# A gated spectral filter beside a two-layer network on one core: new tile blocks, smaller second-layer pieces and a new order of work

## The chip, the cores and the metric

The kernel runs on one core of one Trainium2 chip. The metric is device time in microseconds (us) of one execution; a lower number is better. The kernel before took 148.89 us as the median of 3 runs (148.78, 148.89 and 149.5). Engines are called PE (TensorE, matrix products), DVE (VectorE), ACT (ScalarE), POOL (GpSimd) and SP (SyncE, which here only issues DMAs).

## The reference

The input x has 2048 rows of 640 numbers. Each row is normalized; the normalized matrix goes through a filter in the frequency domain and through a two-layer network, and both results are added to x.

```
def _A_ref(x, w_r, w_i):
    B, S, D = x.shape                                   # 1, 2048, 640
    X = rfft2(x.astype(float32), axes=(-2, -1))
    X = X * (w_r + 1j * w_i)                            # 2048 x 321 weights
    return irfft2(X, s=(S, D), axes=(-2, -1)).astype(bfloat16)

def _B_ref(x, w1, b1, w2, b2):
    h = gelu(einsum("bsd,df->bsf", x, w1) + b1)         # 640 -> 1536
    return einsum("bsf,fd->bsd", h, w2) + b2            # 1536 -> 640

xn = _layernorm(x)
return x + _A_ref(xn, A_w_r, A_w_i) + _B_ref(xn, B_w1, B_b1, B_w2, B_b2)
```

## The kernel before

The 2048 rows are 16 tiles of 128 rows; tile c holds the rows 16p + c of partition p. Everything lies in SBUF at fixed places, PSUM is 8 banks of 512 fp32 columns.

A small planner records every operation with what it reads and writes (`Plan.op`), and two hand-kept tables then fix everything: `ORDER` lists all operations as engine:name, which is the order of each engine's instructions, and `SLOTS` says which of a pool's buffers or PSUM banks each name uses. `Plan.sync` puts in the semaphore waits that these need. An operation waits before its first instruction for all earlier users of its buffers. Nothing is reordered on the chip: an operation that waits holds up all that stands behind it on its engine.

The names in the table, in the order of the data:

- `x`, `w1_hj` (W1 in ten pieces: half h of its 1536 columns, 128-row piece j), `w2_h`, `W..` (the filter), `e`, `m`, `n`, `i`, `g`, `h` (constant tables): loads, all issued by SP one behind the other.
- `st`, `ag`, `ve`, `sq`, `rs`, `nm`: statistics, reciprocal root and normalization of a tile (DVE, the roots on ACT for tiles 0 and 1, on POOL later). `tp`/`tc`: transposition of a normalized tile on PE and its copy to `xnT` (tiles 0 to 5); `td`: the same by a DMA transpose (tiles 6 to 15).
- `h<block>.<fc>.<j>`: first layer, W1 as the stationary operand, a block of tiles from `BLOCKS` as the moving one; `ge`: the gelu on ACT, from PSUM to `gT`. In blocks 0 and 1 (one tile each) a group `h<block>.<q>.<j>` is three 128-column matmuls and needs only piece j of W1.
- `f1`, `f2` (DVE) and `G` (PE), `gx`: folding of a tile and the first step of the transform over rows, copied to `XV`.
- `b` (PE, six groups of 2 or 3 from `GROUPS`), `xb`: transform over columns; its four PSUM banks are emptied by two copies `xb.0` and `xb.1`. `c`, `y`: second step over rows, copied to `Y`. `m`, `z`: products with the filter (into `T`) and their sums (into `Z`), on DVE. `d`, `u`: the first step back, copied to `U`; `vt`: 16 DMA transposes issued by SP, from `U` back to `XV`.
- `e`, `yo`, `y2`, `yf`: transform back over columns (PE), copy and unfolding (DVE). Each `e` needs all 16 `vt`.
- `l`: second layer of a tile into PSUM, `fin`: the last step back over rows added onto it, `os`: plus x and the bias (DVE), `out`: store. For the tiles in `KEEP` the second layer is done early (`k`), added to x (`kk`) and held, and `fin` comes later on its own.
- `xs`: x plus the second bias, `idle0`, `idle1`: matmuls on zeros ahead of the first work.

So the transform is one long chain over PE, ACT, DVE and the DMA transposes, while `h`, `k` and `l` are work of PE that the table places in the chain's waits.

A second-layer sum of 640 columns is written as 512 and 128 columns in two banks (`halves`), evicted by one instruction of 640:

```
def halves(o0, w):
    return [(o0, 512 - o0), (512, o0 + w - 512)] if o0 < 512 < o0 + w else [(o0, w)]
```

All matmuls but the transposes are recorded at line 403, all copies out of PSUM at 413 (ACT) and 414 (DVE), so groups are told apart by their tiles.

Of the kernel before, what the change touches and what calls it, by code (L numbers as in the profile page):

```python
# [7 lines left out]
BF = dt.bfloat16  # L8
F32 = dt.float32
# [4 lines left out]
D = 640  # L14
# [230 lines left out]
BYPE = ()  # L245
# [9 lines left out]
dve:tc1.0 pe:h0.1.2 pe:h0.0.2 act:b1cp sp:g pe:h0.1.3 dve:f10.1 pe:h1.0.0 sp:x8 pe:h0.1.4 pe:h1.0.1 dve:f20.00 pe:h1.1.0 act:ge0.3 sp:x10 pe:h1.1.1
dve:f20.01 act:ge0.4 dve:f20.10 pe:h1.1.2 pe:h1.1.3 sp:x12 pe:h1.1.4 dve:st2.0 pe:h0.0.3 sp:x14 pe:h0.0.4 act:ge1.5 dve:st2.1 pe:h1.0.2 pe:h1.0.3
act:ge0.0 sp:W00m pe:h1.0.4 act:ge0.1 dve:ag2 pe:h1.2.0 dve:st3.1 pe:h1.3.0 act:ge0.2 pe:h1.3.1 sp:W10m act:ge0.5 dve:ve2 dve:st3.0 pe:h1.3.2 pool:rs2
act:ge1.4 pe:h0.2.0 dve:f20.11 act:ge1.2 sp:W12n pe:h0.2.1 dve:ag3 pe:h0.2.2 act:ge1.3 dve:ve3 pe:h0.2.3 dve:nm2 pool:rs3 pe:h1.3.3 sp:W01n pe:h1.3.4
pe:h1.2.1 pe:h0.2.4 act:ge1.10 pool:xbpad1 pe:tp2.0 pool:xbpad0 sp:w2_0 dve:nm3 act:ge1.11 pe:h0.3.0 act:ge1.9 dve:st4.0 pe:h1.2.2 sp:bias2 act:tc2.0
pe:tp3.0 dve:f11.1 pe:h1.2.3 sp:W11n pe:h1.2.4 dve:tc3.0 act:ge1.1 pe:h0.3.1 pe:h0.3.2 act:ge1.7 pe:h0.3.3 dve:f11.0 act:ge1.0 pe:h2.0.0 act:ge0.8  # L260
dve:st6.0 pe:h2.0.3 act:ge0.6 pe:h0.3.4 dve:f21.10 act:ge1.8 pe:h2.4.0 dve:st7.1 act:ge1.6 pe:h2.1.0 sp:W00n act:ge0.7 dve:st7.0 pe:G0 act:ge0.10
pe:h2.2.0 dve:st6.1 pe:h2.1.3 dve:st4.1 pe:h2.8.0 act:ge2.0 dve:st5.0 pe:h2.8.3 pe:G1 act:ge2.1 dve:f21.11 dve:f21.00 pe:h2.9.0 act:ge0.9 dve:st11.0
pe:h2.9.3 act:ge0.11 pe:h2.4.3 act:gx0.0 dve:st5.1 pe:h2.5.0 dve:f21.01 pe:h2.2.3 dve:ag4 dve:ag5 pe:h2.3.0 dve:st8.1 pe:h2.3.3 dve:ve4 dve:ag7
pe:h2.5.3 dve:ag6 pool:rs4 dve:st10.0 pe:h2.6.0 act:ge2.4 dve:ve6 pe:h2.6.3 dve:st13.0 pool:rs6 pe:G2 act:ge2.5 dve:nm4 pe:G3 act:ge2.2 dve:nm5
pe:h2.10.0 act:ge2.3 pe:tp4.0 dve:st14.1 act:ge2.9 pe:tp5.0 dve:nm7 act:tc4.0 pe:h2.10.3 dve:st9.1 pe:h2.11.0 act:tc5.0 dve:f12.0 pe:h2.11.3 pe:h2.7.0
dve:st10.1 pe:h2.7.3 act:ge2.8 dve:nm6 pe:h3.0.0 act:ge2.6 dve:ag10 pe:h3.0.3 dve:st14.0 sp:td6 pe:h3.1.0 act:ge2.7 dve:f12.1 pe:h3.2.0 act:gx1.0
dve:st8.0 pe:h3.2.3 pe:h3.3.0 dve:f22.10 sp:td7 pe:h3.3.3 dve:st9.0 pe:h3.4.0 act:ge3.3 dve:f22.01 pe:h3.4.3 dve:ag8 pe:h3.5.0 act:ge3.2 dve:f22.00
pe:h3.1.3 dve:st13.1 act:ge2.10 pe:h3.5.3 dve:f22.11 act:ge3.1 pe:h3.6.0 dve:ag9 dve:f13.1 pe:G4 act:ge3.0 dve:ve8 pe:h3.6.3 dve:f13.0 act:ge3.4
pool:rs8 pe:h3.10.0 act:ge2.11 dve:st11.1 pe:h3.10.3 pe:G5 act:ge3.5 dve:f23.01 dve:st12.0 pe:h3.11.0 act:gx2.0 dve:nm8 pe:h3.11.3 pe:h3.8.0
dve:f23.00 sp:td8 pe:h3.8.3 dve:nm9 pe:h3.7.0 dve:f23.10 act:ge3.10 pe:h3.7.3 pe:h3.9.0 dve:ag11 dve:f23.11 act:ge3.7 dve:ve10 pe:h3.9.3 dve:f14.1  # L270
# [12 lines left out]
pe:h6.4.0 act:xb2.1 dve:m1.1 pe:h6.4.3 pe:h6.5.0 pe:h6.7.3 act:xb2.0 dve:m0.0 pe:k2.6 dve:m0.1 act:ge6.7 pe:h6.5.3 pe:c1.0 act:ge6.4 dve:z1.1 pe:k2.9
# [38 lines left out]
def bass_parallel_sum__spectral_gfnet__dense_activation_gelu__prompt_kernel(  # L322
# [21 lines left out]
    with ExitStack() as es:  # L344
# [466 lines left out]
```

## Time and profile before

| what | value |
|---|---|
| timed runs | 148.78, 148.89, 149.5 us (median 148.89) |
| the profiled execution: its time, its span | 149.7 us, 148.4 us |
| PE, DVE, ACT busy | 144.8, 110.9, 82.9 us |
| PE clock granted | 1.00 throughout |
| first matmul, last matmul (start) | 0.99 us, 146.2 us |
| first `b` group, first `e` group (PE) | 47.06 us, 105.21 us |

The span runs from the first to the last instruction of the profiled execution, and 1.3 us of that execution lie outside it. Rows of the timeline read: start, length, engine, line, operation, output<-inputs, shape, count, and in brackets the idle time ahead and what ended it. A matmul's length is about 0.2 us longer than the time after which the next one starts, since matmuls overlap: the spacing is (length of a row minus the mean length of one) divided by (count minus one).

### The profile page before, as it was taken

Reading aid. Unit: us, or ns where it says so; the run is one execution under the profiler, and the core shown is the slowest. Engines: PE = TensorE matmul, PEld = TensorE weight load, DVE = VectorE, ACT = ScalarE, POOL = GpSimd, SP = SyncE. Lnnn points to the kernel's source line nnn. Section 1 sums busy time; section 2 is a strip of 40 time slices with the busy share of each in tenths; the row PEclk is TensorE's granted clock in tenths of the full one; section 3 lists DMA queues with packets and bytes.
Section 4 is the critical chain, followed back from the end, with each engine's and each line's share of the span. In section 5 each row is a group of like instructions: output and inputs, shape, how many; then the busy total and the mean of one; then the engine's idle time right before and its main releaser. Section 6 shows DMA issues by size and latency. Waiting matters only on the chain.

```text
span 148.4 us, 4311 instructions
## 1 busy us (share of the span) xinstructions
PE 144.8 (98%) x1847; PEld 99.4 (67%) x1847; DVE 110.9 (75%) x242; ACT 82.9 (56%) x161; POOL 7.0 (5%) x18
## 2 busy tenths in 40 slices
PE   7999999999999999999999999999999999999994
PEld 7989888888868766666554534345676665655564
DVE  2888999999997799498659759700098898968743
ACT  3649889998984775994555467891624204000000
POOL 2003030222200000000000000000000000000000
DMA  4899999366997993004200460645001122101333
GB/s 133 293 326 406 306 269 178 60 93 164 299 203 128 213 210 134 4 4 88 44 4 7 88 133 4 133 92 115 19 4 44 44 88 95 44 0 49 133 111 110
DMA packets 27882, 18.07 MB, mean 122 GB/s; under 512 B 18904, under 2 KB 26584, under 8 KB 27736
## 3 DMA queue, kind: packets, MB, share of 16 engines
q1 hardware_dynamic: 27840, 17.81, 48.8%
q8 instruction: 14, 0.23, 0.6%
q14 instruction: 4, 0.03, 0.1%
q10 hardware_dynamic: 24, 0.00, 0.0%
HBM read 10.92 MB, written 2.62 MB: 91 GB/s over the span
## 4 chain that ended last, share of the span: by engine, by line
PE 70%; DVE 13%; DMA 6%; SPq 5%; issue 2%; ACT 2%; POOL 1%
PE ps L403 70%; DMA X<-in_A_x_dram 6%; SPq L398 5%; DVE stats L508 4%; DVE T L564 3%; DVE T L560 2%; ACT Xb L413 2%; DVE Z L537 1%; DVE mv L510 1%; POOL rstd L519 1%; DVE T L537 1%; DVE ve L518 0%; DVE U L537 0%; DVE W L772 0%
## 5 line engine op out<-in xcount | busy, mean ns | idle before, releaser
L403 PE MATMUL ps<-xnT,W 128*128 128x256 bf16 (+2 forms) x480 | 58.7, 274 | 0.3 <-DMA W<-in_B_w_dram 0.3
L403 PE MATMUL ps<-W,gT 128*128 128x128 bf16 (+4 forms) x408 | 57.9, 291 | 0.0
L403 PEld LDWEIGHTS ps<-xnT,W 128*128 128x128 bf16 x480 | 40.2, 98 | 12.4 <-issue 1.9
L619 ACT ACTIVATE gT<-ps,b1col 128x256 bf16<-128x256 f32 (+2 forms) x96 | 39.3, 483 | 10.8 <-PE ps L403 10.6
L403 PEld LDWEIGHTS ps<-W,gT 128*128 128x128 bf16 x408 | 30.4, 98 | 22.3 <-issue 1.7
L508 DVE BATCH_NORM_STATS2 stats<-X 128x6 f32<-128x320 bf16 x32 | 14.4, 476 | 2.6 <-DMA X<-in_A_x_dram 2.6
L733 DVE TENSOR_TENSOR Wf<-Wf 128x960 bf16<-128x960 bf16 (+1 forms) x12 | 6.8, 597 | 11.8 <-ACT Wf L413 11.7
L413 ACT ACTIVATE Wf<-ps 128x960 bf16<-128x960 f32 (+1 forms) x8 | 6.9, 902 | 12.8 <-PE ps L403 12.8
L413 ACT ACTIVATE Xb<-ps 128x960 bf16<-128x960 f32 (+1 forms) x9 | 9.8, 1138 | 7.0 <-PE ps L403 7.0
L676 DVE TENSOR_TENSOR T<-Y,Wf 128x1288 bf16<-128x1288 bf16 x16 | 12.4, 824 | 0.5 <-ACT Y L413 0.4
L413 ACT ACTIVATE Y<-ps 128x644 bf16<-128x644 f32 x12 | 8.1, 715 | 3.9 <-PE ps L403 3.9
L761 DVE TENSOR_TENSOR xnT<-ps,X 128x640 f32<-128x640 f32 x8 | 6.6, 820 | 4.7 <-PE ps L403 4.7
L772 DVE TENSOR_TENSOR W<-ps,X 128x640 bf16<-128x640 f32 (+2 forms) x10 | 6.9, 687 | 3.8 <-PE ps L403 3.8
L564 DVE TENSOR_TENSOR T<-T 128x512 bf16<-128x512 bf16 (+1 forms) x32 | 9.1, 312 | 0.2
L413 ACT ACTIVATE XV<-ps 128x1280 bf16<-128x1280 f32 x7 | 8.7, 1243 | 0.1
L772 DVE TENSOR_TENSOR W<-ps,xnT 128x640 bf16<-128x640 f32 x8 | 6.5, 820 | 1.8 <-PE ps L403 1.7
L403 PE MATMUL ps<-getab,XV 32*128 32x160 bf16 (+1 forms) x128 | 7.5, 242 | 0.0
L519 POOL TENSOR_TENSOR rstd<-ve,mhalf 128x2 f32<-128x2 f32 (+1 forms) x8 | 6.1, 763 | 31.1 <-DVE ve L518 31.1
L738 DVE TENSOR_TENSOR Wf<-Wf 128x960 bf16<-128x960 bf16 (+1 forms) x12 | 6.7, 596 | 0.8 <-PE ps L403 0.7
L403 PEld LDWEIGHTS ps<-getab,XV 32*128 32x128 bf16 (+1 forms) x128 | 6.4, 146 | 1.2
L403 PE MATMUL ps<-etab,XV 32*128 32x160 bf16 (+1 forms) x128 | 7.2, 232 | 0.0
L680 DVE TENSOR_TENSOR Z<-T 128x644 bf16<-128x644 bf16 x16 | 7.0, 488 | 0.1
(52 smaller groups left out, 111.6 us busy)
## 6 DMA issues: line engine op xcount, KB each, us to landing
out_dram<-W SPq DMA_DIRECT2D x15, 160.0 KB, 1.8
X<-in_A_x_dram SPq DMA_DIRECT2D x7, 320.0 KB, 8.2
W<-in_B_w_dram SPq DMA_DIRECT2D x10, 192.0 KB, 5.6
W<-in_B_w_dram SPq DMA_DIRECT2D x2, 960.0 KB, 8.7
Wf<-in_A_w_i_dram SPq DMA_DIRECT2D x7, 160.5 KB, 3.9
Wf<-in_A_w_r_dram SPq DMA_DIRECT2D x7, 160.5 KB, 4.5
gtab<-c_G SPq DMA_DIRECT2D x1, 512.0 KB, 7.8
htab<-c_H SPq DMA_DIRECT2D x1, 512.0 KB, 5.0
```

Of the source, the lines that this page charges most:

```text
L398: return K.op(name, q, lambda e, _: e.dma_start(dst, src), reads=reads, writes=[buf], after=after, dma=sem or name, gate=gate)
L403: ins = e.matmul(o_, lhsT=lw, rhs=rh, start=st, stop=sp_, skip_group_check=True)
L413: return e.activation(dst(), src(), ACT.Copy)
L508: K.op(f"st{c}.{h}", "dve", lambda e, _, c=c, h=h: e.bn_stats(stats[:, c, 6 * h:6 * h + 6], view(X, c * D + H2 * h, [[1, H2]])), reads=[B_ ...
L519: K.op(f"rs{c0}", "pool", lambda e, _, a=a, b=b: e.tensor_tensor(out=rstd[:, a:b], in0=ve[:, a:b], in1=mhalf[:, a:b], op=ALU.pow), reads=[ ...
L564: ring_ops.append(K.op(f"f2{pair}.{k}{i}", "dve", lambda e, _, op=op, x1v=x1v, xfv=xfv, o_=o_, o0=o0, o1=o1, w=w: e.tensor_tensor(out=xfv( ...
L619: K.op(f"ge{bi}.{fc}", "act", lambda e, _, c0=c0, nt=nt, fc=fc, f0=f0, hps=hps: e.activation(gT[:, fc, 128 * c0:128 * (c0 + nt)], psb(hps. ...
L676: filt_ops.append(K.op(f"m{pair}.{k}", "dve", lambda e, _, k=k, Y=Y, TB=TB, pair=pair: e.tensor_tensor(out=view(TT, TB.slot * 8 * KP + k * ...
L680: K.op(f"z{pair}.{r}", "dve", lambda e, _, TB=TB, Z=Z, r=r, op=op: e.tensor_tensor(out=view(Zb, Z.slot * 4 * KP + r * KP, [[2 * KP, 2], [1 ...
L733: K.op(f"y2{gi}.{k}", "dve", lambda e, _, k=k, op=op, yo=yo, y2=y2, n=n: e.tensor_tensor(out=view(Wf, Y2 + y2.slot * 3 * D + (H2 - 1) * k, ...
L738: K.op(f"yf{gi}.{k}", "dve", lambda e, _, k=k, op=op, y2=y2, yf=yf, n=n: e.tensor_tensor(out=view(Wf, YF + yf.slot * 3 * D + (D - 1) * k, ...
L772: K.op(f"os{c}.{o0}", "dve", lambda e, _, c=c, os_=os_, fps=fps, o0=o0, w=w, kept=kept, base=base, home=home if kept else None: e.tensor_t ...
```

## The change

- `BLOCKS`: tiles 8 to 15 are two blocks of four instead of two blocks of two and one of four.
- The normalization of tile 0 is two instructions, columns 384 to 639 first, and the transposes and copies of each part wait for that part alone.
- The second layer, `fin`, `kk` and `os` work in pieces of 384 and 256 columns, one bank each; tile 15 keeps pieces of 320, 160 and 160.
- The product with the real filter part is written over `Y`, and the sums `z` over that; `Z` is gone. With the memory freed there are six `Y`, four `Xb` and four `U` buffers in place of two, two and three, some of them in tables that are used up by then.
- `GROUPS` are cut elsewhere (still 3, 3, 2, 3, 3, 2 tiles in some order), `idle0` has 38 matmuls instead of 42.
- `ORDER` and `SLOTS` are new in all their lines.

```diff
-BLOCKS = [(0, 1), (1, 1), (2, 2), (4, 2), (6, 2), (8, 2), (10, 2), (12, 4)]
+BLOCKS = [(0, 1), (1, 1), (2, 2), (4, 2), (6, 2), (8, 4), (12, 4)]
-GROUPS = [(0, 2), (2, 3), (5, 3), (8, 3), (11, 3), (14, 2)]
+GROUPS = [(0, 3), (3, 3), (6, 2), (8, 3), (11, 3), (14, 2)]
+CUTS = [(0, 384), (384, 256)]
-WARM = (42, 4)
+WARM = (38, 4)
...
-pe:tp0.3 sp:w1_13 pe:idle1 dve:tc0.0 dve:nm1 sp:w1_14 pe:h0.1.0 pe:h0.1.1 act:tc0.3 dve:f10.0 sp:x4 pe:h0.0.0 pe:tp1.0 sp:x6 pe:h0.0.1 pe:b1mm
-dve:tc1.0 pe:h0.1.2 pe:h0.0.2 act:b1cp sp:g pe:h0.1.3 dve:f10.1 pe:h1.0.0 sp:x8 pe:h0.1.4 ...
+dve:f10.0 pe:h0.1.0 act:tc0.3 sp:x4 pe:h0.1.1 dve:f10.1 pe:h0.1.2 act:tc1.0 pe:h0.0.0 sp:x6 pe:h0.1.3 dve:f20.01 dve:f20.10 pe:h0.0.1 act:b1cp
+pe:h0.1.4 sp:g dve:f20.00 pe:h0.0.2 pe:h1.0.0 ...
...
-        p_xn, p_x1, p_xf, p_xb, p_y, p_t, p_z, p_u = [Pool(k, n) for k, n in (
-            ("xn", 5), ("x1", 1), ("xf", 2), ("xb", 2), ("y", 2), ("t", 2), ("z", 2), ("u", 3))]
+        p_xn, p_x1, p_xf, p_xb, p_yz, p_t, p_u = [Pool(k, n) for k, n in (
+            ("xn", 4), ("x1", 1), ("xf", 2), ("xb", 4), ("yz", 6), ("t", 2), ("u", 4))]
...
+                parts = ((0, 384), (384, D)) if c == 0 else ((0, D),)
+                for (a, b), B_part in zip(parts, B_xn):
+                    norm = K.op(f"nm{c}" if not a else f"nm{c}.3", "dve", lambda e, _, c=c, n=n, a=a, b=b, xnv=xnv: e.tensor_scalar(
+                        out=xnv(n, a, [[1, b - a]]), in0=view(X, c * D + a, [[1, b - a]]), ...
...
+            m0 = K.op(f"m{pair}.0", "dve", lambda e, _: e.tensor_tensor(out=yv(Y, False), in0=yv(Y, False), in1=wv(pair, 0), op=ALU.mult),
+                reads=[Y, B_w, B_wpad], writes=[Y], after=[m1])
+                    rows = view(TT, yz(Y) + r * KP, [[2 * KP, 2], [1, KP]])
+                    return e.tensor_tensor(out=rows, in0=rows, in1=view(TT, TB.slot * 4 * KP + r * KP, [[2 * KP, 2], [1, KP]]), op=op)
...
-                            (psb(ps_.slot, [[1, b]], a - base), gT[:, fc, 128 * c:128 * c + 128], W2[:, fc, a:a + b], fc == 0, False)
-                            for fc in range(f0, f0 + 3) for a, b in halves(o0, w)],
+                            (psb(ps_.slot, [[1, w]]), gT[:, fc, 128 * c:128 * c + 128], W2[:, fc, o0:o0 + w], fc == 0, False)
+                            for fc in range(f0, f0 + 3)],
...
+                    for o0, w in CUTS:
+                        kps = K.buf(f"kps{c}_{o0}", psum, 1, HIGH)
+                        second(f"k{c}.{o0}", c, kps, o0, w, free)
...
-                for o0, w in PIECES.get(c, [(0, D)]):
+                for o0, w in PIECES.get(c, CUTS):
```

The instructions move in many places. Three of them matter here. Line 410 after the change is line 403 before it, 420 is 413, 566 is 549 and 704 is 700.

**The start, on DVE and PE.** Before, DVE up to the normalization of tile 0:

```order
L508 BN_STATS stats<-X 128x6 x3
L510 BN_AGGR mv<-stats 128x2
L508 BN_STATS stats<-X 128x6
L514 RECIPROCAL rstd<-ve 128x1
L510 BN_AGGR mv<-stats 128x2
L537 TENSOR_SCALAR Z<-X,mv,rstd 128x640
```

After it:

```order
L520 BN_STATS U<-X 128x6 x2
L522 BN_AGGR mv<-U 128x2
L520 BN_STATS U<-X 128x6 x2
L526 RECIPROCAL rstd<-ve 128x1
L522 BN_AGGR mv<-U 128x2
L552 TENSOR_SCALAR T<-X,mv,rstd 128x256
L552 TENSOR_SCALAR T<-X,mv,rstd 128x384
```

The aggregate of tile 0 stands one statistic earlier, the reciprocal stands behind the same four statistics, and the normalization is in two. On PE in the same place, before (`EB` in the new names holds the zeros and the identity that were `warm` and `ident`):

```order
L549 MATMUL ps<-ident,Z 128x128 x5
L403 MATMUL ps<-warm 128x128 x4
L403 MATMUL ps<-xnT,W 128x128 x9
L549 MATMUL ps<-ident,Z 128x128 x5
L403 MATMUL ps<-xnT,W 128x128 x3
L403 MATMUL ps<-ident,b1t 128x12
L403 MATMUL ps<-xnT,W 128x128 x84
```

and after:

```order
L566 MATMUL ps<-EB,T 128x128 x2
L410 MATMUL ps<-EB 128x12
L566 MATMUL ps<-EB,T 128x128 x3
L410 MATMUL ps<-EB 128x128 x4
L566 MATMUL ps<-EB,T 128x128 x5
L410 MATMUL ps<-xnT,W 128x128 x96
```

The transposes of tile 1 and the small bias transpose now stand ahead of all first-layer matmuls. Among these, `h0.1.4`, the first to need the fifth piece of W1, was the ninth group of three (24 matmuls ahead of it) and is the seventh (18 ahead).

**Groups 4 and 3 of the column transform, on PE and ACT.** `etab` (after: `EB`) with 24 matmuls of 160 columns is a group of three tiles. Before, PE between groups 3 and 4:

```order
L403 MATMUL ps<-etab,XV 128x160 x24
L403 MATMUL ps<-W,gT 128x512
L403 MATMUL ps<-W,gT 128x128
```

(nine such pairs in all stand there), and after, where group 4 comes ahead of group 3:

```order
L410 MATMUL ps<-EB,XV 128x160 x24
L410 MATMUL ps<-W,gT 128x384 x6
L410 MATMUL ps<-xnT,W 128x512 x5
L410 MATMUL ps<-EB,XV 128x160 x24
```

ACT has both copies of the first of the two groups there, before and after; after:

```order
L638 ACTIVATE gT<-ps,b1col 128x512
L420 ACTIVATE Xb<-ps 128x3x2x160 x2
L638 ACTIVATE gT<-ps,b1col 128x512
L420 ACTIVATE Xb<-ps 128x3x2x160
```

What stands between the two groups on PE is shorter than before.

**The DMA transposes to `XV`, on SP.** After the change the 16 of them stand in one row behind all loads:

```order
L405 DMA htab<-c_H 128x2048
L405 DMA getab<-c_GE 128x800
L704 DMA_TRANSPOSE XV<-gtab 128x5x128
L704 DMA_TRANSPOSE XV<-T 128x5x128 x2
L704 DMA_TRANSPOSE XV<-gtab 128x5x128
L704 DMA_TRANSPOSE XV<-U 128x5x128 x4
```

They stood behind the loads before as well. What differs is which instruction they wait for: the first of them needs the second copy to `U` of pair 1 (`u1.1`), and on PE all four `d` of the first four pairs now come together (`d0.0`, `d1.1`, `d0.1`, `d1.0`), behind the `c` of six pairs; before, `d0` came behind the `c` of four and `d1` some 13 us later.

More of the change, by code (lines that the diff above doesn't have):

```diff
@@ L255 @@
[L255 to L258, printed above, removed]
@@ L317 @@
[L317 to L318 removed]
+idle0:0 b1ps:0 xn0:0 x10:0 xf0:0 tps0.0:2 tps0.3:1 idle1:3 tps1.0:4 aps0:0 xn1:1 x11:0 xf1:1 tps2.0:6 tps3.0:4 aps1:0 xn2:2 x12:0 xf2:0 tps4.0:5
+tps5.0:3 aps2:0 xn3:3 x13:0 xf3:1 aps3:0 xn4:0 x14:0 xf4:0 aps4:0 xn5:1 x15:0 xf5:1 aps5:0 xn6:2 x16:0 xf6:0 aps6:0 xn7:3 x17:0 xf7:1 aps7:0 hps0_0:6
@@ L454, in first @@
             chain.append(o)
[L455 removed]
+        table.gate.append(load("bias1", "act", b1t, b1v, B_b1))
         first(load_x(0, 1))
```

359 lines of the change are left out of this document (188 added, 171 removed).

## The prediction

> **What bounds the kernel now.** I read the busy times of the engines first, then the table of waits, then PE's timeline at each place where its matmuls are not back to back.
>
> ```profile
> span 148.4 us, 4311 instructions
> PE 144.8 (98%) x1847; PEld 99.4 (67%) x1847; DVE 110.9 (75%) x242; ACT 82.9 (56%) x161; POOL 7.0 (5%) x18
> ...
> PEld ps L403 <- issue: 4.5, 19, 0.3
> ...
> PEld ps L403 <- ACT Xb L413: 1.3, 4, 0.5
> ```
>
> PE is busy for 98% of the span, and in the table of waits no other engine holds it for more than 1.3 us in all. Busy time alone proves little, since matmuls overlap, so I look at spacings:
>
> ```profile
> 28.41 1.80 PE L403 MATMUL ps<-xnT,W 128*128 128x256 bf16 x15
> 97.19 4.49 PE L403 MATMUL ps<-xnT,W 128*128 128x512 bf16 x20
> 8.97 1.24 PE L403 MATMUL ps<-xnT,W 128*128 128x128 bf16 x19 [0.27 <-DMA W<-in_B_w_dram]
> ...
> L403 PE MATMUL ps<-xnT,W 128*128 128x256 bf16 x300 | 37.0, 273 | 0.0
> L403 PE MATMUL ps<-xnT,W 128*128 128x512 bf16 x60 | 14.1, 380 | 0.0
> L403 PE MATMUL ps<-xnT,W 128*128 128x128 bf16 x120 | 8.1, 222 | 0.3 <-DMA W<-in_B_w_dram 0.3
> ```
>
> (1.80 - 0.273)/14 = 109 ns for 256 columns, (4.49 - 0.380)/19 = 216 ns for 512, (1.24 - 0.222)/18 = 56 ns for 128: PE streams columns at one rate with about 2 ns for each matmul on top. From the first transposes to the last matmul it does little else. So the change can gain only the matmuls it removes and the holes it closes, and loses every hole it opens. These are the holes that I find, beside the one in the third row above:
>
> ```profile
> 21.38 0.88 PE L549 MATMUL ps<-ident,Z 128*128 128x128 bf16 x10
> 22.10 1.15 PE L403 MATMUL ps<-xnT,W 128*128 128x256 bf16 x9
> ...
> 39.75 0.38 PE L403 MATMUL ps<-xnT,W 128*128 128x256 bf16 x2
> 40.21 0.45 PE L403 MATMUL ps<-gtab,T 128*128 128x128 bf16 x5
> ...
> 59.00 0.38 PE L403 MATMUL ps<-xnT,W 128*128 128x256 bf16 x2
> 59.64 0.50 PE L403 MATMUL ps<-Xb,mtab 32*32 32x322 bf16 x32 [0.26 <-ACT Xb L413]
> ```
>
> Ten transposes need 0.56 and took 0.72 (0.16 lost); two matmuls need 0.22 and took 0.46 (0.24 lost, at `G13`) and 0.64 (at `c1.0`: 0.42, of which some 0.1 is what any such step of 32 small matmuls costs on entry, so 0.31). Together 0.71 us, and nothing that the new order must bring back.
>
> **The change part by part.** *Matmuls.* Tiles 8 to 11 as one block: 120 matmuls of 256 columns become 60 of 512, 60 x (218 - 216) ns = 0.12 us less. Pieces of 384 and 256: the same 640 columns in two matmuls; 384 is not in the trace, between 109 and 216 ns it is half way, 163, and 163 + 109 = 272 = 216 + 56, so nothing. Tile 15's last piece:
>
> ```profile
> 144.81 0.99 PE L403 MATMUL ps<-W,gT 128*128 128x160 bf16 x12
> 145.71 0.65 PE L403 MATMUL ps<-W,gT 128*128 128x32 bf16 x12
> 146.20 0.24 PE L403 MATMUL ps<-Wf,htab 128*128 128x32 bf16 x2
> ```
>
> Six pairs of 32 and 128 columns took 0.49 us, 82 ns each; one matmul of 160 is (0.99 - 0.23)/11 = 69. Thirteen pairs save 0.17 us. The four zero matmuls less stand ahead of the first transposes, which wait for DVE: nothing. Sum: -0.29.
>
> *The start.*
>
> ```profile
> 4.27 0.19 DVE L510 BATCH_NORM_AGGREGATE mv<-stats 128x2 f32<-128x12 f32 x1
> 4.38 0.44 DVE L508 BATCH_NORM_STATS2 stats<-X 128x6 f32<-128x320 bf16 x1
> 4.82 0.16 DVE L514 RECIPROCAL rstd<-ve 128x1 f32<-128x1 f32 x1
> 5.02 0.45 DVE L537 TENSOR_SCALAR Z<-X,mv,rstd 128x640 bf16<-128x640 bf16 x1
> ```
>
> The aggregate moves ahead by one statistic, but the reciprocal still stands behind all four, so it starts at about 4.8 as before. Half of the normalization is ready some 0.2 us sooner, and tile 1's transposes fill a time in which PE had stood before. This buys nothing, since PE then waits for the fifth piece of W1, the end of the 0.27 us idle in the row at 8.97. The loads are issued in the same order, so I let it land at the same time. Then 18 first-layer matmuls are done by then and not 24; the transposes of tile 1 and the bias were done before as well. Six matmuls of 56 ns: +0.33. Bounds: 0, if the piece comes a microsecond sooner, and +0.5.
>
> *`tc3` on ACT.* The copy of tile 3 now stands on ACT behind that of tile 2, and the next 256-column matmul needs both. Before, DVE had it:
>
> ```profile
> 13.63 0.71 ACT L413 ACTIVATE xnT<-ps 128x640 bf16<-128x640 bf16 x1
> 14.13 0.48 DVE L414 COPY xnT<-ps 128x640 bf16<-128x640 bf16 x1
> ```
>
> It ends about 0.2 us after PE has run out of one-tile matmuls. +0.2 (0 to 0.4).
>
> *Evacuation in the middle.* `b` and `d` need all four low banks empty, so the two copies must fit beneath the matmuls placed between.
>
> ```profile
> 68.69 2.62 PE L403 MATMUL ps<-W,gT 128*128 128x512 bf16 x18
> 68.81 2.37 ACT L413 ACTIVATE Xb<-ps 128x960 bf16<-128x960 f32 x2 [1.87 <-PE ps L403]
> 71.23 1.12 PEld L403 LDWEIGHTS ps<-etab,XV 128*128 128x128 bf16 x24 [0.25 <-ACT Xb L413]
> ```
>
> Between groups 3 and 4, 2.55 us of matmuls just covered two copies on ACT (0.12 + 2.37 + 0.06). In the new order the cover is six matmuls of 384 and five of 512, 0.98 + 1.08 = 2.06 us, and both copies are on ACT again: a hole of 0.5 (0.1 to 0.7). By the same count ahead of `b1` (three gelus stand ahead of the second copy on ACT) about 0.25, and at `d1.1`, both copies of `d0.0` on ACT beneath twelve matmuls of 384 (1.95 us), about 0.15. Together +0.9, bounds 0.2 to 1.5. The other steps of the middle come out with 0 to 0.2 us to spare.
>
> *More evictions.* Eight `kk` and fifteen `os` become two instructions each.
>
> ```profile
> L772 DVE TENSOR_TENSOR W<-ps,X 128x640 bf16<-128x640 f32 x7 | 5.7, 819 | 1.7 <-PE ps L403 1.7
> L772 DVE TENSOR_TENSOR W<-ps,X 128x160 bf16<-128x160 f32 x2 | 0.7, 325 | 0.6 <-PE ps L403 0.6
> L772 DVE TENSOR_TENSOR W<-ps,X 128x320 bf16<-128x320 f32 x1 | 0.5, 492 | 1.4 <-PE ps L403 1.4
> ...
> 120.00:130.00 10.00, 10.00 (x99) 6.25 (x97) 8.81 (x13) 1.83 (x2) 0.00 (x0) 1.00 0.23 83
> 130.00:146.50 16.50, 16.44 (x146) 10.36 (x144) 10.72 (x18) 0.00 (x0) 0.00 (x0) 1.00 0.23 83
> ```
>
> From 160 and 320 columns: 1.04 ns a column and 158 ns fixed, of which about 80 overlap with the next one (the aggregate row above is 0.19 long and the next starts after 0.11). So a second instruction costs 0.08 to 0.16 us, 17 of them in the tail 1.4 to 2.7 us. The two rows of the tail leave DVE 1.2 + 5.8 us free. I take nothing; without that cover it is rival D. The Trainium skill (Perfetto Trace Analysis, Optimizing Scalar/DVE Operations) has a rule against this part: each VectorE instruction on PSUM carries about 125 ns, and grouping pays where the engine is saturated; by it the 17 would cost an estimated 2.1 us of DVE, inside the bounds just given.
>
> *In place.*
>
> ```profile
> L676 DVE TENSOR_TENSOR T<-Y,Wf 128x1288 bf16<-128x1288 bf16 x16 | 12.4, 824 | 0.5 <-ACT Y L413 0.4
> L680 DVE TENSOR_TENSOR Z<-T 128x644 bf16<-128x644 bf16 x16 | 7.0, 488 | 0.1
> ...
> 60.00:80.00 20.00, 20.00 (x367) 12.12 (x352) 14.29 (x24) 13.94 (x26) 0.00 (x0) 1.00 0.14 27
> 80.00:105.00 25.00, 24.99 (x355) 11.50 (x354) 13.09 (x24) 15.99 (x31) 0.00 (x0) 1.00 0.44 87
> ```
>
> `m` and `z` keep their count, shapes and types, and I take the same time for them. A slower write over an input has no row; a tenth of these 19.4 us would be 1.9 us in a middle where DVE is busy for 27.4 of 45 us.
>
> *Sum.* -0.71 - 0.29 + 0.33 + 0.2 + 0.9 = +0.4 us of span: 148.4 becomes 148.8, and the profiled time 149.7 becomes 150.1. That execution lay 0.8 above the median of its own runs, so on the median 148.9 + 0.4 = 149.3. My holes are counted where a copy just misses, and a copy that is late once leaves the next one time; I take half of the 0.4 and say **149.1**.
>
> **The rivals.** *B, the old holes go and no new ones open.* For it: the new holes are each a few tenths, less than one eviction, and the piece of W1 that I let land late may not. Against it: the table gives ACT both copies at two of the places. Then -0.71 - 0.29 = -1.0: 147.9.
>
> *C, slower: the transposes to `XV` hold up the first `e`.*
>
> ```profile
> 99.51 2.60 SPq L700 DMA_TRANSPOSE XV<-gtab  x2
> 102.15 1.28 SPq L700 DMA_TRANSPOSE XV<-U  x1
> 103.58 1.79 PE L403 MATMUL ps<-W,gT 128*128 128x512 bf16 x12
> 105.21 0.95 PE L403 MATMUL ps<-getab,XV 128*128 128x160 bf16 x12
> ...
> XV<-gtab SPq DMA_TRANSPOSE x6, 2.6
> ```
>
> Two issues take 2.64 us of SP, 1.32 each, and one lands 2.6 after its start: before, the last landed some 0.4 us ahead of the first `e`. Now all sixteen follow `u1.1` in one row: about 0.9 us from the end of `d0.1` to the end of that copy, then 15 x 1.32 + 2.6, together 23.3. Beneath it PE has, from `d0.1` to the first `e`, 60 matmuls of 512, 21 of 384, 27 of 256, a group of 0.95 and seven steps of about 0.52: 12.96 + 3.42 + 2.94 + 0.95 + 3.64 = 23.9 us. From the point where one of the copies to `U` that they wait for is over 0.6 us late, each microsecond moves the end, and nothing is left to fill it. With 1.6 us late, 149.1 + 1.0 = 150.1. Against it: DVE and ACT are busy for 13.1 and 16.0 of the 25 us there.
>
> *D, slower: DVE becomes the bound of the tail.* If the 1.4 to 2.7 us fall where `fin` waits for `yf`, half to all of the smaller figure: 149.8 to 150.5, say 150.3. Against it: the free time above.
>
> That the two-part normalization doesn't bring PE's first real work forward is my forecast already, at no cost.
>
> **How the numbers follow.** Forecast (holes close and others open, within 0.7 us of before): 0.45; B 0.25; C 0.21; D 0.09. About 0.5%, 0.74 us, is what a measurement of this kernel can tell from no change, so faster means below 148.15: B, 0.25. Within: 0.45. Slower, above 149.63: C and D, 0.30. The bounds of the unknown costs (0 to 0.5, 0 to 0.4, 0.2 to 1.5) put the forecast's own case between 148.2 and 149.9 on the median; cut where the other cases begin, its own range is 148.2 to 149.6. With B and most of C and D, cutting a tenth at either end, 147.8 to 150.4.
>
> **What would show it.** PE's first idle time in the new profile: ended by the DMA of W1, longer than 0.27 us, at 8.9. In PE's waits: `Xb` and `U` copies on ACT ahead of groups `b1` and `b3` and of `d1.1`, 0.2 to 0.5 us each. No hole at `G13`. The first `e` between 104.9 and 105.7 us with the last transpose landing just ahead of it; if it starts more than a microsecond after the last matmul ahead, C is right. In the tail PE without idle time, DVE busier by about 1.4 us. The last matmul at 146 to 147 us. The forecast is wrong if PE has over 3 us of holes in all, or under 0.7.

## The result, and the profile after

| | time, us | runs | profiled execution (span) |
|---|---|---|---|
| predicted | 149.1 (147.8 to 150.4) | | |
| kernel before | 149.0 median (148.78 to 149.5) | 6 | 149.7 (148.4) |
| changed kernel | 150.54 median (149.96 to 151.98) | 6 | 150.41 (149.1) |

The changed kernel is slower: 1.0109 of the time before, 95% interval 1.0061 to 1.0157, some 1.6 us. Every ratio here and below compares the fast runs of the two kernels alone, so it can differ a little from the quotient of two medians. The six runs of the changed kernel spread over 2.0 us and those of the kernel before over 0.7; but 11 and 21 further runs of the kernel before, beside the experiments, spread over 1.7 each (148.85 to 150.59 and 148.83 to 150.53), so the spread sets the two kernels apart no further. The first rows of the changed kernel's page:

```profile
span 149.1 us, 4174 instructions
PE 143.5 (96%) x1770; PEld 100.5 (67%) x1770; DVE 114.6 (77%) x265; ACT 79.2 (53%) x150; POOL 6.9 (5%) x24
```

PE has less to do (143.5 against 144.8) and a longer span to do it in. The table of waits names a releaser that held PE in none of the rows of before:

```profile
PEld ps L410 <- DMA XV<-U: 1.4, 1, 1.4
...
PE ps L410 <- DMA XV<-U: 1.1, 1, 1.1
...
PEld ps L410 <- DMA W<-in_B_w_dram: 0.5, 1, 0.5
...
PE ps L410 <- ACT Xb L420: 0.3, 1, 0.3
```

It is one wait, ahead of the first `e`. PE's timeline (start, duration, idle time ahead in brackets) at the places of the prediction:

```profile
6.54 1.19 PE L410 MATMUL ps<-xnT,W 128*128 128x128 bf16 x18
8.06 1.35 PE L410 MATMUL ps<-xnT,W 128*128 128x128 bf16 x21 [0.34 <-DMA W<-in_B_w_dram]
...
52.00 1.26 PE L410 MATMUL ps<-xnT,W 128*128 128x256 bf16 x10
53.24 0.93 PE L410 MATMUL ps<-EB,XV 128*128 128x160 bf16 x11
...
67.38 1.24 PE L410 MATMUL ps<-xnT,W 128*128 128x512 bf16 x5
68.94 1.25 PE L410 MATMUL ps<-EB,XV 128*128 128x160 bf16 x20 [0.32 <-ACT Xb L420]
...
76.19 1.46 PE L410 MATMUL ps<-W,gT 128*128 128x384 bf16 x8
77.58 0.51 PE L410 MATMUL ps<-T,ntab 32*32 32x320 bf16 x32
...
103.66 0.49 PE L410 MATMUL ps<-W,gT 128*128 128x256 bf16 x3
105.22 1.42 PE L410 MATMUL ps<-getab,XV 128*128 128x160 bf16 x24 [1.07 <-DMA XV<-U]
...
146.41 0.23 PE L410 MATMUL ps<-Wf,htab 128*128 128x160 bf16 x1
```

With 109 ns a matmul of 256 columns, PE was free at 103.66 + 3 x 0.109 = 103.99 and started `e0` at 105.22: **1.23 us lost**. At the other end, the last matmul starts at 146.41 and the span ends 2.7 us later; before, 148.4 - 146.20 = 2.2. The other rows are read against the prediction below.

Why the transposes are late shows in SP's timeline and in the row of landing times (for the tile `XV`) of the changed kernel:

```profile
80.69 1.25 SPq L704 DMA_TRANSPOSE XV<-gtab  x1
81.98 2.59 SPq L704 DMA_TRANSPOSE XV<-T  x2
84.61 1.28 SPq L704 DMA_TRANSPOSE XV<-gtab  x1
85.93 6.17 SPq L704 DMA_TRANSPOSE XV<-U  x4
92.15 1.61 SPq L704 DMA_TRANSPOSE XV<-T  x1
93.80 2.60 SPq L704 DMA_TRANSPOSE XV<-gtab  x2
96.44 1.28 SPq L704 DMA_TRANSPOSE XV<-T  x1
97.77 6.04 SPq L704 DMA_TRANSPOSE XV<-U  x4
```
```profile
DMA to landing us min/median/max: 2.6/2.7/4.6
```

The same row of before reads:

```profile
DMA to landing us min/median/max: 2.6/2.6/2.7
```

At 1.28 an issue and 0.03 between, four take 5.21 us; here two groups of four took 6.17 and 6.04, and a single one 1.61. That is 0.96 + 0.83 + 0.33 = 2.1 us more than sixteen undisturbed issues. The window of the DMA records from 86.0 to 90.6 us, in 40 slices of 0.115 us, shows what happens in the first of them (first row: busy tenths of the DMA engines; second: what they moved; then the queues):

```profile
DMA  9999981000399999990000000010000039999990
GB/s 218 236 220 200 198 161 29 0 0 0 76 200 209 196 203 178 60 149 0 0 0 0 0 0 0 0 9 9 9 9 9 11 62 253 285 289 292 247 237 3
...
q8 instruction: 1, 0.02, 1.3%
```

Two transposes' bursts run at about 200 GB/s. In the 18th slice, at 88.05, comes one packet of the instruction queue, 16 KB; it takes 0.96 us in its record, and for 1.6 us next to nothing is moved. The page counts 14 such packets in either kernel, one for some 126 of 1770 matmuls of the changed one, as if they carried PE's program; x2, x3 and x8 below test that. In the trace of the changed kernel they stand at 80.05, 88.05, 91.73 and 98.74 in this stretch: the first ahead of the row, three in it. In that of before they stand at 80.74, 89.55 and 97.82, each at a gap between two groups of transposes.

### The profile page after: what moved, and what is told of

Same layout as the page of the kernel before. It is cut to its first block, busy times and chain, and to the rows that moved or that the text cites. A ratio compares the mean times of both kernels' runs of the same rounds, so it can differ in the third digit from the quotient of the medians.

```text
span 149.1 us, 4174 instructions
## 1 busy us (share of the span) xinstructions
PE 143.5 (96%) x1770; PEld 100.5 (67%) x1770; DVE 114.6 (77%) x265; ACT 79.2 (53%) x150; POOL 6.9 (5%) x24
## 4 chain that ended last, share of the span: by engine, by line
PE 74%; SPq 10%; ACT 6%; DMA 5%; DVE 2%; issue 1%; DVEq 0%
PE ps L410 74%; SPq L704 8%; DMA W<-in_B_w_dram 3%; ACT gT L638 3%; DMA XV<-U 2%; SPq L405 2%; ACT Xb L420 2%; DVE W L802 2%; ACT xnT L420 1%; ACT gtab L420 0%; ACT T L420 0%; PE ps L566 0%; DVEq L224 0%
## 5 line engine op out<-in xcount | busy, mean ns | idle before, releaser
L410 PE MATMUL ps<-W,gT 128*128 128x256 bf16 (+3 forms) x396 | 59.4, 296 | 0.0
L520 DVE BATCH_NORM_STATS2 U<-X 128x6 f32<-128x320 bf16 x32 | 13.9, 474 | 2.8 <-DMA X<-in_A_x_dram 2.8
L420 ACT ACTIVATE T<-ps 128x644 bf16<-128x644 f32 (+2 forms) x17 | 9.7, 613 | 5.7 <-PE ps L410 5.7
L420 ACT ACTIVATE XV<-ps 128x1280 bf16<-128x1280 f32 (+1 forms) x8 | 9.6, 1196 | 2.8 <-PE ps L410 2.8
L802 DVE TENSOR_TENSOR W<-ps,X 128x256 bf16<-128x256 f32 (+3 forms) x17 | 7.6, 466 | 3.6 <-PE ps L410 3.4
L792 DVE TENSOR_TENSOR xnT<-ps,X 128x256 f32<-128x256 f32 (+1 forms) x16 | 7.6, 484 | 2.1 <-PE ps L410 2.1
L583 DVE TENSOR_TENSOR T<-T 128x128 bf16<-128x128 bf16 (+1 forms) x32 | 8.9, 313 | 0.1
L410 PE MATMUL ps<-Wf,htab 128*128 128x256 bf16 (+3 forms) x33 | 7.5, 295 | 0.0
L698 DVE TENSOR_TENSOR T<-T 128x644 bf16<-128x644 bf16 x16 | 7.3, 486 | 0.1
L579 DVE TENSOR_TENSOR T<-T 128x640 bf16<-128x640 bf16 x16 | 7.3, 481 | 0.1
```

What stands on the lines that cost most here:

```text
L410: ins = e.matmul(o_, lhsT=lw, rhs=rh, start=st, stop=sp_, skip_group_check=True)
L420: return e.activation(dst(), src(), ACT.Copy)
L520: K.op(f"st{c}.{h}", "dve", lambda e, _, c=c, h=h: e.bn_stats(stats[:, c, 6 * h:6 * h + 6], view(X, c * D + H2 * h, [[1, H2]])), reads=[B_ ...
L579: K.op(f"f1{pair}.{k}", "dve", lambda e, _, k=k, op=op, xnv=xnv, x1v=x1v: e.tensor_tensor(out=x1v(H2 * k, [[D, 2], [1, H2]]), in0=xnv(0, 0 ...
L583: ring_ops.append(K.op(f"f2{pair}.{k}{i}", "dve", lambda e, _, op=op, x1v=x1v, xfv=xfv, o_=o_, o0=o0, o1=o1, w=w: e.tensor_tensor(out=xfv( ...
L698: return e.tensor_tensor(out=rows, in0=rows, in1=view(TT, TB.slot * 4 * KP + r * KP, [[2 * KP, 2], [1, KP]]), op=op)
```

## The experiments

Ratios are to the kernel before, run beside each kernel; "F" is the theory of the instruction packets, "Q" that a long row backs up by itself, "U" that two of the source tensors are slow. All names stand in the order tables.

**x1_early_d0**: `d0` and its transposes ahead of `b3` and `c2`.

```
 pe:b4 ... -pe:b3 +pe:d0.0 ... +pe:d0.1 ... +pe:b3 ... pe:c2.1 ... pe:c2.0 ... -pe:d0.0 pe:d1.1 -pe:d0.1
```

> The changed kernel with d0.0 and d0.1 (and so the first four transposes to XV) ahead of b3 and c2 instead of behind them; nothing else moves on PE but the banks' users. If the unbroken row of sixteen transposes is what costs: PE's wait ahead of e0 falls from 1.1-1.2 us to under 0.5, and the time from 150.5 to 149.3-149.8 (1.002 to 1.006 of before). If the loss lies in the wait at b3, in the more numerous VectorE instructions or in the last output: e0's wait may go, but the time stays at 150.3-150.8.

151.82, 1.018 (1.0118 to 1.0242). PE did not wait for `XV` any more: six transposes were late, but the last landed at 106.81, just as PE got to `e0` (106.52 + 3 x 0.109 = 106.85). VectorE was late elsewhere: 0.46 us ahead of `d1.0` and 0.91 ahead of `b5`, both ended by copies to `U` on DVE that I had put behind its products, and 1.09 at 20 us for a normalization that the edit doesn't touch. Inconclusive: the edit made waits of its own.

**x2_phase_after**: the idle matmuls ahead of everything halved in width and doubled in number.

```
-WARM = (38, 4)        psb(b.slot, [[1, 128]]), warm, warm
+WARM = (76, 4)        psb(b.slot, [[1, 64]]), warm, warm[:, 0:64]      (idle0 alone)
```

> The changed kernel with its 38 idle matmuls of 128 columns as 76 of 64: the same PE time, 38 PE instructions more ahead of everything. Theory F (a 16 KB instruction packet of PE that meets a transpose makes it land 1.4-1.9 us late): the packets of 88.05, 91.73 and 98.74 come at about 86.3, 90.2 and 95.2, and the transposes in flight there are the late ones (those issued at about 84.6-86, 88.6-89.9 and 93.8-95), while the one issued at 97.8 lands in 2.7 us unless a packet stands there. Theory Q (a long row of transposes backs up by itself): the fifth to eighth and the thirteenth and fourteenth stay the late ones. Theory U (sources in U2 and U3): vt6, vt7, vt13 stay late. Time 149.8 to 151 under each.

151.54, 1.0154 (1.011 to 1.0198). The packets came at 86.13 and 90.19, as expected, and at 97.22, 2 us later than expected. The late transposes were the 4th to 7th and 10th to 12th (those issued at 85.06 to 90.14 and 95.15 to 97.78, landing after 3.2 to 4.6 us), where the changed kernel has the 5th to 9th and 13th to 14th; the one issued at 99.62 took 2.65. Three of them now had `gtab` as their source, which in the changed kernel none had. So the late ones moved with the packets, as F says and Q and U do not. PE lost 1.4 us ahead of `e0` (0.33 of matmuls from 104.52, `e0` at 106.28), and the time came out above the 149.8 to 151 expected under each theory.

**x3_minus_before**: the kernel before, 21 idle matmuls of 256 columns for 42 of 128.

> The kernel before with its 42 idle matmuls of 128 columns as 21 of 256: the same PE time, 21 PE instructions fewer ahead of everything, no transpose moved. Theory F: packets at about 68.4, 82.9 and 102.1 instead of 66.4, 80.7 and 97.8; the transposes in flight there (vt0 or vt1, vt4, and vt13 or vt12) land over 3.2 us after their issue, the last one at 105.5-106.5 instead of 104.8, PE waits 0.5-1.5 us ahead of e0, and the time is 149.3-150.3 (1.002 to 1.009). Theories Q and U: all sixteen still land in 2.6-2.7 us, no wait ahead of e0, 149.0 within 0.3.

150.81, 1.0104 (1.0066 to 1.0142): slower by more than F said, and not where. The packets near the transposes hardly moved (66.32, 81.23, 97.83; one from 89.55 to 90.97) and all sixteen transposes landed within 2.7 us. The later packets did move, from 108.61, 119.83 and 133.58 in the first profile of before to 111.31, 122.57 and 136.44. In its profile DVE stood 1.97 us in the tail, waiting for an output, and PE 0.62 us behind it:

```profile
139.40 0.82 DVE L772 TENSOR_TENSOR W<-ps,xnT 128x640 bf16<-128x640 f32 x1 [1.97 <-DMA out_dram<-W]
```
```profile
141.08 0.45 PE L403 MATMUL ps<-Wf,htab 128*128 128x512 bf16 x2 [0.62 <-DVE Wf L738]
```

That output, issued at 135.36, had met a packet at 136.44 and landed at 139.31. So 21 PE instructions fewer, with no work moved, cost this kernel 1%. For the transposes the run decides nothing. Up to `e0` (105.13, before 105.21) its profile lost nothing against the first profile of before; its last matmul started at 146.9 instead of 146.2, of which the 0.62 is the most. Where the rest of the 1.7 us between the medians went stays open.

**x4_xb4_dve**: `act:xb4.0` becomes `dve:xb4.0`, ahead of `m3.1`.

> The changed kernel with the copy xb4.0 on DVE (ahead of m3.1) instead of ACT. The wait of 0.58 us at b3 falls under 0.2. If the row of transposes starts with PE, all of it moves up by 0.4-0.5 us and the time falls to 149.9-150.2 (1.006 to 1.008); if the end is set by something that PE's middle doesn't move, it stays at 150.4-150.6.

152.11, 1.018 (1.0138 to 1.0222). A miss of mine: the wait at `b3` went, and `xb3.0`, behind four products and a sum on DVE, came late instead; PE waited 1.06 us ahead of `c2.1`, everything behind moved by 0.8, and PE idled 0.9 ahead of `e0`.

**x5_swap_d**: `d0.1` and `d1.1` exchanged with their copies, so the row starts sooner and has a gap.

```
 pe:d0.0 ... -pe:d1.1 ... act:u2.1 dve:u3.1 ... pe:d0.1 ... act:u1.1 dve:u0.1
 pe:d0.0 ... +pe:d0.1 ... act:u1.1 dve:u0.1 ... pe:d1.1 ... act:u2.1 dve:u3.1
```

> The changed kernel with d0.1 and d1.1 exchanged (with their four copies), so that the first transpose to XV can start some 1.6 us sooner and the row has a gap before its last eight; no other work moves. If the row of transposes, lengthened by the instruction packets that meet it, is what the end waits for: PE's wait ahead of e0 falls from 1.1-1.2 us to 0-0.4 and the time from 150.5 to 149.3-149.8 (1.002 to 1.005 of before). If something else costs (b3's wait, VectorE in the tail, the last outputs): e0 comes sooner, but the time stays within 0.3 of 150.5.

**x9_tail**: x5_swap_d, and `out15.320` on ACT's queue.

> x5_swap_d with the last output but one issued by ACT's queue instead of SP's. In the changed kernel three outputs stood in a row on SP and the last was issued 0.46 us after its data was ready. Expected: out15.480 issued within 0.1 us of its data, the end 0.3 to 0.45 us after that of x5_swap_d measured from the last matmul (2.7 us becomes 2.3), the time 0.3-0.4 less than x5_swap_d. If the output's landing is set by the queue of writes and not by its issue, no difference.

**x8_before_p52**: the kernel before, 94 idle matmuls of 56 columns for 42 of 128.

> The kernel before with 94 idle matmuls of 56 columns instead of 42 of 128: as much PE time, 52 more PE matmuls ahead of everything, no other edit. Theory F (packets are tied to PE's instruction count and delay the transposes they meet): the packet of 97.8 comes at about 94.6, that of 108.6 at about 102, among the last four transposes; one of them lands over 3.2 us after its issue, the last at 105.5-106.7 instead of 104.8, PE waits 0.4-1.6 us ahead of e0, and the time rises by 0.4-1.6 us. Theories Q (a long row backs up) and U (sources): all sixteen land in 2.6-2.7 us, no wait at e0, 149.0 within 0.3.

**x0_after_again**: the changed kernel.

> The changed kernel once more, as the control of this call. Theory F: the packets at 80, 88, 91.7 and 98.7 again, and the same five or six transposes late; 150.0-151.0. If the late landings were an accident of one execution, another pattern and e0 at another time.

x0_after_again, the control, gave 1.0106 (1.0061 to 1.0152), with packets at 79.86, 87.63, 92.05 and 99.21, again seven late transposes, and `e0` 0.77 us late (104.62 - 103.52 - 3 x 0.109): the pattern is no accident. x5_swap_d gave 150.39, 1.0073 (1.0034 to 1.0112). That is above the range expected; it is 0.5 us less than the control by the ratios, but their intervals overlap, so a gain is not shown by the time. In its profile `e0` came 0.2 us after PE was free. x9_tail gave 150.24, 1.0061 (1.0031 to 1.0091), 0.15 less than x5_swap_d, which is inside the noise too. Its profiled execution had a packet 1.1 us into the row, eight late transposes and 1.26 us lost at `e0`, with the same order as x5_swap_d up to there: whether a packet falls just ahead of the row or into it changes from execution to execution, and with it the wait. Its end came 2.3 us after the last matmul (148.9 - 146.60) instead of 2.7 (148.4 - 145.69), as expected, although the times do not resolve this.

x8_before_p52 is the sharpest of them: 1.0048 (1.0009 to 1.0087), and no transpose was moved. PE's timeline and the DMA window from 101.5 to 105 (slices of 0.0875 us):

```profile
104.14 1.79 PE L403 MATMUL ps<-W,gT 128*128 128x512 bf16 x12
106.44 0.78 PE L403 MATMUL ps<-getab,XV 128*128 128x160 bf16 x8 [0.51 <-DMA XV<-U]
```
```profile
DMA  9999983009004999999999000001000001019302
GB/s 211 219 222 214 222 167 71 9 0 187 0 0 91 199 208 214 199 202 187 138 41 9 0 0 0 0 0 9 9 9 9 9 9 12 9 29 249 36 0 61
...
q8 instruction: 1, 0.02, 2.7%
```

The packet came at 102.36 (expected: about 102); the one expected at 94.6 came at 91.91, ahead of its group. The transpose issued at 101.31 landed after 4.25 us, the last one at 106.40, and `e0` started at 106.44. The twelve matmuls ahead of it are those that took 105.21 - 103.58 = 1.63 us in the kernel before, so PE was free at 105.77: 0.67 us lost. Seven of the sixteen were late, in groups of three to five: no long row is needed. PE also waited 0.9 us for pieces of W1 (0.3 in the kernel before), so the 0.5% need not be the transposes' alone. The transposes to `XV` of fourteen profiles, by where a packet starts after their issue (two whose landing the trace does not tell are left out, and so is y4_search below, where a load of 512 KB stood among them and two landed after 4.5 and 5.4 us with no packet in this time):

| packet starts after the issue by | transposes | landing over 2.9 us |
|---|---|---|
| 0 to 2.25 us | 49 | 49 |
| 2.25 to 2.7 us | 16 | 4 |
| none in this time | 157 | 19, each issued directly behind one of the late ones above |

**x10_no_vt_after** and **x11_no_vt_before**: both kernels without the sixteen transposes, whose results the inverse stage then lacks.

> The changed kernel without its sixteen transposes from U to XV (the inverse stage then reads what lies in XV; all other work is kept). If the transposes cost the changed kernel its time: no wait ahead of e0, 149.0-149.4 (1.000 to 1.003 of before), 1.2 us less than with them, and a narrower spread of runs. If something else does: 150.2 or more.

> The kernel before without the same sixteen transposes. They cost it little (e0 stood 0.4 us behind the last landing and PE had no wait there): 148.6-149.1 (0.997 to 1.000). The two kernels without transposes then stand within 0.5 us of one another. If the transposes cost it as much as the changed kernel: 147.8.

> The kernel before once more, for a second profile. Its first profile was 0.8 us above the median of its runs. Theory F: the packets near 66, 81, 90 and 98 again, in the gaps between the groups of transposes, no wait at e0; 148.8-149.3 if the first profile's extra 0.8 lay in one wait elsewhere, which this one would then not show.

149.96, 1.0041 (1.0006 to 1.0076), and 149.66, 1.0021 (0.9996 to 1.0047). Both are above their ranges, and the runs of x10 spread no less than those of the changed kernel (149.03 to 151.13). By the ratios the two kernels stand 0.3 us apart without the transposes and 1.6 apart with them, so about 1.3 us of the loss are theirs, give or take 1.0: that is the root of the summed squares of the half-widths 0.0048, 0.0035 and 0.0026 of the three intervals, 0.0065. In x10 PE had no wait at `e0`. The 0.3 is itself the sum of two larger things, as the last matmul of x10 and that of x11 (second row) show:

```profile
144.72 0.23 PE L409 MATMUL ps<-Wf,htab 128*128 128x160 bf16 x1
```
```profile
145.85 0.24 PE L402 MATMUL ps<-Wf,htab 128*128 128x32 bf16 x2
```

Without the transposes PE of the changed kernel is done 1.1 us sooner than PE of the kernel before. But the end comes 3.9 us after its last matmul (148.6 - 144.72) and 2.4 after that of before (148.3 - 145.85), since in x10 `os15` stood waiting for a slot:

```profile
145.32 0.95 DVE L799 TENSOR_TENSOR W<-ps,X 128x320 bf16<-128x320 f32 x3 [1.10 <-DMA out_dram<-W]
```

The slot was that of `out10.0`, issued at 140.99 and landed at 145.23. A packet's record begins at 143.03, 0.3 us after such an output usually lands (1.8 us after its issue); that this packet held it is not shown. The kernel before again, **x12_before_again**, took 149.03, with no transpose late and no wait at `e0`. It also had no wait for the fifth piece of W1, which in the first profile of before had cost PE 0.45 us (8.97 - 7.85 - 12 x 0.056, with the row of 12 at 7.85), and its last matmul started at 145.54 instead of 146.20.

**y4_search** and **z31_search**: x9_tail with its order between `b0` and the first `fin` (in z31_search, to the end) searched anew, by the durations of the profile and with packets that hold what they meet.

> x9_tail with the order between b0 and the first fin searched anew: the engines' durations are the profile's, and each packet of PE's instructions is taken to hold a transpose that it meets by 1.7 us and the next issue by up to 1.1, at several places near the counts seen. Estimate: 2 us less than x9_tail by these durations, so 148.0-149.0 (0.993 to 1.000 of before), with PE's wait ahead of e0 under 1 us. If the durations don't carry over to another order, 149.5-150.5.

> x9_tail with the order between b0 and the last output searched anew, by the profile's durations, with a packet that holds what it meets at twelve places near the counts seen, the loads left where they were, and every accumulation begun by the part that starts it (in y4_search 28 were not, so a part of those sums was lost there and only its time can be read). Estimate by these durations: 2 us less than x9_tail, 148.0-149.0, 0.993 to 0.999 of before, with PE's wait ahead of e0 under 0.5 us. If y4_search was fast for its broken sums: 149.5-150.5.

149.3, 0.9977 (0.9943 to 1.001), and 149.15, 0.9988 (0.9965 to 1.0011): both medians are just above the 148.0 to 149.0 expected, and neither kernel is told apart from the kernel before. In y4_search 28 parts of accumulations stand out of order, and where the part that starts a sum isn't first, what came ahead of it is lost; z31_search has all sums whole. In both, PE's wait at `e0` is gone (0.2 us or less), the last matmul starts at 144.7 and 144.9. In z31_search what is left stands at the end:

```profile
DVE W L802 <- DMA out_dram<-W: 2.1, 1, 2.1
```

In z31_search the span ends 148.2 - 144.89 = 3.3 us after the last matmul. DVE had stood 2.1 us for the landing of `out9.0`, which met a packet at 140.46, and the last output stood behind four others.

**x13_after_tail**: the changed kernel with `out15.320` on ACT's queue, and no other edit.

> The changed kernel with one edit: the last output but one issued by ACT's queue, so that the last output does not stand behind it on SP. Theory: 0.46 us of the changed kernel's loss is this row of outputs, the rest is the wait for the transposes. Expected: out15.480 issued within 0.1 us of its data, 2.2-2.3 us from the last matmul to the end instead of 2.7, and the time 0.3-0.5 us less than the changed kernel's (1.007 to 1.008 of before instead of 1.0106 to 1.0109). If the time stays at 1.0106 or more, the outputs are not part of the loss.

150.84, 1.0093 (1.006 to 1.0126): not told apart from the changed kernel. The profile says why. The last output was issued with its data, but all three pieces of tile 15 were late:

```profile
146.11 0.99 PE L410 MATMUL ps<-W,gT 128*128 128x160 bf16 x12
146.94 0.23 PE L410 MATMUL ps<-Wf,htab 128*128 128x160 bf16 x1
```
```profile
147.26 0.95 DVE L802 TENSOR_TENSOR W<-ps,X 128x320 bf16<-128x320 f32 x3 [0.82 <-PE ps L410]
```

The row on DVE names PE, but the `fin` for the first of these stands ahead of the matmuls at 146.11. `out10.0`, whose slot `os15` takes, was issued at 143.21, met the packet of 144.36 and landed at 147.17. Five of the nine profiles with this order of the tail (the changed kernel twice, x4, x10 and x13; not x1, x2, x5 and x9) have `out10.0` landing late, at 145.2 to 147.2.

**z31b_outs**: z31_search with another end.

```
-os13:0 os14:3                       +os13:3 os14:0
-sp:out15.0 sp:out12.0 sp:out14.0    +sp:out12.0 (behind os12.384) act:out14.0 sp:out15.0
```

> z31_search with the end rearranged: out12.0 issued as soon as its data is there, out14.0 on ACT's queue, and the slots of os13 and os14 exchanged, so that os14 no longer waits for the landing of out9.0 (which a packet at 140.5 held to 143.5). In z31_search the last matmul stood at 144.9 and the end 3.2 us behind it, 0.9 of it in four outputs on SP's queue. Expected: the last output issued within 0.15 us of its data, the end 2.1-2.4 us behind the last matmul, the time 0.7-1.0 us less: 148.2-148.6 (0.992 to 0.996 of before). If another output meets the packet and holds a slot, 148.8-149.2.

**148.22 median of 12 (147.9 to 148.97), 0.9935 (0.9909 to 0.9962)**: faster than both kernels, and 0.8 us less than z31_search by the ratios, as expected and with intervals that do not meet. Since z31_search moves most of the order, its distance to the changed kernel doesn't tell what the transposes alone are worth. Eight of the transposes of z31b_outs are late, and `e0` starts 0.2 us after PE is free:

```profile
103.33 0.98 PE L410 MATMUL ps<-W,gT 128*128 128x256 bf16 x6
104.14 1.38 PE L410 MATMUL ps<-getab,XV 128*128 128x160 bf16 x24
...
145.47 0.23 PE L410 MATMUL ps<-Wf,htab 128*128 128x160 bf16 x1
```

The end comes 2.2 us after the last matmul.

The Trainium skill (DMA: Bandwidth & Descriptors, Rules for kernel authors) says that spreading transfers over the issuing engines brings no bandwidth and only saves issue time. The traces agree on the issue time: with `out15.320` on ACT's queue the last output of x9 was issued 0.03 us after its data, instead of 0.46 in the changed kernel. No run here measures bandwidth.

## Why the prediction was wrong

**The step that failed** is the one that priced the transposes. Rival C named the mechanism and the place; its arithmetic was "15 x 1.32 + 2.6, together 23.3" against 23.9 us of matmuls, and I read the 0.6 between them as slack and gave the case 0.21. By the sign named for it (`e0` more than a microsecond late) C is what came. The cover was right: PE was free at 103.99, 24.2 us after the end of `d0.1` at 79.79. The chain was not: the last transpose landed at 105.17, 25.4 us after it. Its rows of before had shown one spacing and one landing time, because there every packet fell into a gap between two groups, and I took them as fixed. In an unbroken row of 22 us three packets have no gap to fall into; they add 2.1 us. The condition that I gave, that one of the copies to `U` is late by over 0.6 us, was the wrong place to look: the copies were in time.

**The end was not in the sum at all.** I wrote that the last matmul would come at 146 to 147, which it does (146.41), and took what follows as before. It takes 2.7 us instead of 2.2: the order has three outputs in a row on SP, and the last was issued 0.46 us after its data. In the control it is more (149.1 - 145.79 = 3.3), since there `os15` also stood 0.77 us, with `out10.0` landing at 145.98. How much of the median this makes is open: x13 did not resolve it.

**The sum for PE came out too high.** It said that PE would be done 0.4 us later than before. Without the time lost at `e0` the last matmul would stand at 146.41 - 1.23 = 145.18, 1.0 us sooner than the 146.20 of before; in the control and the second profile of before 145.79 - 0.77 - 145.54 = -0.5, and without the transposes 144.72 - 145.85 = -1.1. That is near rival B's -1.0. So that x10 and x11 stand 0.3 us apart, about the +0.4 of the sum, is luck: PE gained and the end lost. In the first pair of profiles 0.9 of the 1.4 us too much lie in the start, where the 25th first-layer matmul started at 8.97 before and at 8.06 + 6 x 0.056 = 8.40 after, a gain of 0.57 where I said a loss of 0.33. The rest I can't place. So the 0.7 us between the first two profiles (spans of 149.1 and 148.4) are -1.0 for PE, +1.2 at `e0` and +0.5 at the end; the 1.3 between the control and the second profile of before (149.1 and 147.8) are -0.5, +0.8 and +1.0.

**What held.** Single terms of the sum, by the rows of the profile after: at `b3` 68.94 - 67.38 - 5 x 0.216 = 0.48 (said 0.5); at `b1` 53.24 - 52.00 - 10 x 0.109 = 0.15 (0.25); at `d1.1` 77.58 - 76.19 - 8 x 0.163 = 0.09 (0.15); matmuls of 384 columns at 163 ns, (1.46 - 0.32)/7, as taken. In the start PE lost 8.06 - 6.54 - 18 x 0.056 = 0.5 at the fifth piece of W1, but the piece landed 0.9 us sooner than in the first profile of before; since the second profile of before has no such wait, this term depends on the execution more than on the change. The old holes at `G13` and `c1.0` are closed. Written over their inputs, the sums take the time they took, 486 ns against 488:

```profile
L698 DVE TENSOR_TENSOR T<-T 128x644 bf16<-128x644 bf16 x16 | 7.3, 486 | 0.1
```

Rival D did not come: DVE is busy for 1.8 us more from 130 us on (10.72 became 12.52, inside the 1.4 to 2.7 named), and PE has no idle time there.

```profile
130.00:146.70 16.70, 16.64 (x140) 12.65 (x138) 12.52 (x30) 0.00 (x0) 0.00 (x0) 1.00 0.21 75
```

**Halving the sum** went the right way for PE and not far enough. But its argument, that a late copy gives the next one time, is about copies. What cost the time was a chain on another queue and the end, and nothing behind these made up for it.

## What to carry to other kernels

A chain of transfers that is hidden with less than a microsecond to spare is not hidden: add up how long it lasts with each packet of instructions that it must meet (here 0.1 to 1.4 us of issue each, one packet to some 126 matmuls), and leave a gap or start it sooner by that much. Don't judge a sum by the total that it gives: here two errors of about a microsecond stood against one another, and only the profile, taken stage by stage, tells them apart. And follow the last matmul to the end: queue the last outputs apart, and give no late tile the slot of an output that has just been issued (together 0.8 us between z31_search and z31b_outs).

## What the runs showed of the hardware

A 16 KB packet of the instruction queue, 0.9 to 1.8 us in its record, stops the transposes under way: in the two windows above 200 GB/s fell to 0 to 29 for 1.6 and 1.3 us. All 49 transposes with a packet in the first 2.25 us after their issue landed late, and the late ones landed after 2.9 to 4.6 us instead of 2.6 to 2.7; outputs under way landed after up to 4.1 instead of 1.9 (`out9.0` of z31_search). The packets follow PE's instruction count: 52 matmuls more ahead of all work moved the packet of 108.0 (1471 matmuls before it in the second profile of before) to 102.36 (1461 before it), with a cost of 0.5% (0.1 to 0.9) to a kernel that was otherwise unchanged, and 21 fewer moved that of 108.61 (1485 before it) to 111.31 (1482). But the count is not exact, as the packets of x3 that did not move show, and the same program meets them within about a microsecond of one place in one execution and the next. Why a packet of 0.96 us should stop the transposes for 1.6, these runs don't show.
